# A new order for all work and loads of a state-space scan with a low-rank mixer, with 29 units of unread identity products ahead of 15 words in place of 14 ahead of 5

## The chip, the cores and the metric

One core of a Trainium2 chip runs the kernel. The engines named below are TensorE (PE, with its weight loads PEld), VectorE (DVE), ScalarE (ACT), GpSimd (POOL) and SyncE (SP), which issues all DMAs here. Each engine works off its own queue strictly in the order in which the program wrote it, and waits on semaphores for the others. The metric is the device time of one execution in microseconds; the median of several runs is given.

## The reference

Two blocks follow each other. The first is a chunked state-space scan (Mamba2 SSD) for 4 batches, 8 heads, 768 positions, head dimension 32 and state dimension 16. Its output, with the heads side by side, is the input `x` of the second, a mixer of 256 channels.

```python
# scan, per chunk of 32 positions; cum = cumsum(log a) inside the chunk
M = (Cc @ Bc.T) * exp(cum_i - cum_j) * causal
y = M @ xc + (Cc @ state) * exp(cum)
state = exp(sum(la)) * state + (Bc * decay_from_j).T @ xc
# mixer, per batch
h = x.T @ U @ V                       # rank 32, over the 768 positions
u = x + h.T
out = u + relu(u @ w_ch1) @ w_ch2     # 256 -> 1024 -> 256
```

a, B, C and x are float32. U, V and the two weights come as float64 and are turned into float32 on the chip.

## The kernel before

The scan's work is cut into twelve pairs of 128-position blocks, k = 0 to 11, three pairs to a batch. The mixer works on each batch in three blocks of 256 positions, j = 0 to 2, and takes the hidden layer in quarters, i = 0 to 3. Blocks 0 and 1 of batch 0 use plain float32 products; all others split each factor into parts near, far and both, whose products run at the faster float32r rate.

The order of everything is written out by hand in `PLANS` (lines 36 to 72). `PLANS[0]` holds the first loads. `PLANS[1]` is one list of words, and `follow` (line 1063) calls one function for each word, in order. What a word emits goes to the end of each engine's queue. So the list fixes, for every engine at once, what stands ahead of what. In words of the scan the first number is the pair minus 3 (`s-3` is pair 0, `s8` pair 11); in words of the mixer it is 1 minus the batch (`d1.0` is batch 0, block 0; `d-2.2` is batch 3, block 2).

- Loads: `B` and `X` load a pair's B with C, and its x; `L` does both for the pair of its number plus 3. `Z` loads U and V, `w0` to `w8` the words of the weights. SyncE issues them in the order of the list. The first transfer of a `B`, `X`, `L` or `w` word is also held until the last VectorE instruction written ahead of it has ended (`until`, `begin`, line 195).
- Weights: `c` (three steps for each number) turns loaded words into float32. c0 is U and V, c1 to c5 are w_ch1, c6 to c9 are w_ch2. `R` (two steps each) splits them into near, far and both.
- Scan: `A` and `K` make the decays (F, FD, kept) of all batches from the logarithms `la`. `Q` and `P` scale B and C into BC on VectorE, `E` and `D` make the decayed B (on POOL for batch 0, on VectorE after). `V` and `T` transpose BC into T and Cm; for pairs from 6 on that goes over DRAM, in two calls. `g` multiplies them, `m` and `M` mask the result on VectorE, `s` and `u` make the states. `i`, `j` and `n` add up the output, `y` copies it out, and `t` and `O` transpose it for the mixer.
- Mixer: `v` spreads U and V, `p` projects and `x` multiplies with V, `a` adds h to x (VectorE). `U` is a plain hidden quarter, `f`, `e` and `h` are the split one, `S` splits a block of u. `d` is a step of the second product; its later steps add u and store.
- `F` sets a number of identity products that the next tile in PSUM gets ahead of its own work. Nobody reads them. The tags w, x and z have 2, 3 and 3 PSUM banks.

```python
    def idle(t, n):
        while n > 0:
            m = min(n, max(t.shape[1] // P, 1), 4)
            w = min(P, t.shape[1])
            nc.tensor.matmul(out=t[:, :m * w].rearrange("p (m i) -> p m i", i=w), lhsT=ident,
                             rhs=ident[:, None, :w].to_broadcast([P, m, w]), start=True, stop=True)
            n -= m
    def bank(tag, *dims):
        t = psum.tile([P, *dims], FP32, tag=tag, name=tag, bufs=BANKS[tag])
        if fills[0]:
            idle(t if len(dims) == 1 else t.rearrange(
                {2: "p a b -> p (a b)", 3: "p a b c -> p (a b c)"}[len(dims)]), fills[0])
        fills[0] = 0
        return t
```

One unit is one product of the 128 by 128 identity with 128 columns of itself, in float32, which the profile shows as two records.

## Time and profile before

| | us |
|---|---|
| runs | 214.29, 214.87, 216.78 |
| median | 214.87 |
| profiled execution, span from first to last instruction | 212.4 |
| TensorE busy | 202.9 |
| weight loads busy | 180.9 |
| VectorE busy | 173.2 |
| ScalarE busy | 121.0 |
| POOL busy | 6.3 |

The profile is of one execution. It gives its span; the device time of that execution lies around the span, and the median of the runs is 2.5 us above it. A row of a timeline reads: start in us from the start of the span, length in us, engine, line, operation, what it writes and reads, shape, how many records were merged, and in brackets how long the engine was idle ahead of it and what it waited for. Lines of VectorE often read L170, since one helper issues them; there the tile names tell the words apart. TensorE's records overlap, so the start of the next row tells more of the time that a row takes than its own length.

### The profile page before, as it was taken

What the parts mean: (1) busy time and instruction counts of PE and PEld (TensorE: products, weight loads), DVE (VectorE), ACT (ScalarE), POOL (GpSimd) and SP (SyncE); (2) the same over time, 40 slices, a digit from 0 to 9 for tenths busy, and PEclk for the clock granted to TensorE, in tenths of its full rate; (3) what the DMA queues carried; (4) which work ended last, traced back from release to release, by engine and by line L of the source; (5) the groups of instructions that cost most, each with busy time, mean ns of one, the idle gap of its engine ahead of it and who ended that gap; (6) DMA issues with size and microseconds to landing.
All of it is one profiled execution on the core that took longest, in us unless ns stands there. A gap on an engine that the chain in (4) does not pass through costs nothing.

```text
span 212.4 us, 7511 instructions
## 1 busy us (share of the span) xinstructions
PE 202.9 (96%) x3190; PEld 180.9 (85%) x3190; DVE 173.2 (82%) x363; ACT 121.0 (57%) x279; POOL 6.3 (3%) x22
## 2 busy tenths in 40 slices
PE   7988889999999999999999999899999999999994
PEld 5765666878979997988999999589998999999993
DVE  4299979999899999999799995777986299859941
ACT  3354668489969746285588361669713565554310
POOL 4022000000000000000000000000000000000000
PEclk9999999999999999999999999999999999999999
DMA  5997799994751488356755766626510000324354
GB/s 82 138 150 160 89 246 181 190 241 121 102 71 31 79 207 130 88 83 83 108 89 94 149 143 132 112 38 122 117 52 0 0 5 0 49 32 71 49 102 99
DMA packets 120177, 21.43 MB, mean 101 GB/s; under 512 B 110096, under 2 KB 118352, under 8 KB 120144
## 3 DMA queue, kind: packets, MB, share of 16 engines
q1 hardware_dynamic: 120144, 20.95, 53.9%
q8 instruction: 25, 0.41, 0.9%
q14 instruction: 8, 0.07, 0.2%
HBM read 14.39 MB, written 6.55 MB: 99 GB/s over the span
## 4 chain that ended last, share of the span: by engine, by line
PE 75%; DVE 8%; issue 4%; DMA 4%; ACT 3%; SPq 3%; POOL 0%; POOLq 0%; DVEq 0%; ACTq 0%
PE x L846 35%; PE z L846 28%; DMA bc<-in_B_dram 4%; SPq L196 3%; DVE words L170 2%; PE x L584 2%; PE z L739 1%; PE w L803 1%; PE x L714 1%; PE x L739 1%; DVE S L170 1%; ACT yT L759 1%; PE x L815 1%; DVE o L170 1%; DVE BC L170 1%
## 5 line engine op out<-in xcount | busy, mean ns | idle before, releaser
L170 DVE SCALAR_TENSOR_TENSOR words<-words 128x512 fp32r<-128x512 f32 (+6 forms) x60 | 39.4, 669 | 2.4 <-ACT words L420 0.8
L846 PE MATMUL x<-words,w 128*128 128x256 f32 x288 | 38.1, 280 | 0.0
L846 PEld LDWEIGHTS x<-words,w 128*128 128x128 f32 x288 | 34.9, 188 | 1.6 <-issue 1.2
L846 PE MATMUL x<-u,w 128*128 128x256 f32 x240 | 34.3, 282 | 0.0
L846 PE MATMUL z<-u,w 128*128 128x256 f32 x240 | 32.7, 278 | 0.0
L851 ACT ACTIVATE x<-x 128x512 f32<-128x512 f32 (+1 forms) x27 | 15.5, 577 | 28.2 <-PE x L846 26.4
L846 PEld LDWEIGHTS x<-u,w 128*128 128x128 f32 x240 | 30.3, 188 | 0.6 <-ACT yT L759 0.2
L846 PEld LDWEIGHTS z<-u,w 128*128 128x128 f32 x240 | 29.7, 188 | 0.1
L851 ACT ACTIVATE z<-z 128x512 f32<-128x512 f32 (+1 forms) x24 | 13.7, 574 | 12.3 <-PE z L846 10.2
L846 PE MATMUL z<-words,w 128*128 128x256 f32 x144 | 19.6, 280 | 0.0
L846 PEld LDWEIGHTS z<-words,w 128*128 128x128 f32 x144 | 17.7, 188 | 0.9 <-issue 0.9
L170 DVE SCALAR_TENSOR_TENSOR words<-x,words 128x512 fp32r<-128x512 f32 x20 | 13.6, 682 | 4.5 <-ACT words L886 4.4
L170 DVE SCALAR_TENSOR_TENSOR words<-z,words 128x512 fp32r<-128x512 f32 x20 | 13.6, 682 | 2.2 <-ACT words L886 2.2
L886 ACT ACTIVATE words<-x 128x512 fp32r<-128x512 f32 x20 | 12.0, 598 | 3.3 <-PE x L846 3.2
L170 DVE TENSOR_TENSOR yT<-x,yT 128x384 f32<-128x384 f32 (+1 forms) x15 | 9.2, 613 | 5.1 <-PE x L846 2.7
L170 DVE TENSOR_TENSOR BC<-bc,F 128x512 f32<-128x512 f32 (+2 forms) x18 | 8.7, 508 | 5.4 <-DMA bc<-in_B_dram 3.0
L886 ACT ACTIVATE words<-z 128x512 fp32r<-128x512 f32 x20 | 11.8, 597 | 1.7 <-PE x L846 1.2
L170 DVE SCALAR_TENSOR_TENSOR S<-S,kept,w 128x64 f32<-128x64 f32 x40 | 11.2, 279 | 1.7
L584 PE MATMUL x<-Cm,T 32*64 32x128 f32 x192 | 11.6, 307 | 0.6 <-DVE Cm L170 0.4
L651 ACT ACTIVATE Sm<-S,slot 128x128 f32<-128x128 f32 (+1 forms) x18 | 6.0, 385 | 9.9 <-DVE S L170 9.9
L584 PE MATMUL z<-Cm,T 32*64 32x128 f32 x192 | 10.5, 307 | 0.0
L170 DVE TENSOR_TENSOR M<-x,causal 128x256 int32<-128x256 int32 x24 | 9.1, 421 | 1.6 <-PE z L584 1.6
(152 smaller groups left out, 363.5 us busy)
## 6 DMA issues: line engine op xcount, KB each, us to landing
words<-in_moe_w_ch_dram SPq DMA_DIRECT2D x7, 512.0 KB, 5.5
squares<-w1f SPq DMA_DIRECT2D x52, 64.0 KB, 1.9
x<-in_x_dram SPq DMA_DIRECT2D x24, 128.0 KB, 4.1
out_dram<-o SPq DMA_DIRECT2D x32, 64.0 KB, 2.3
bc<-in_B_dram SPq DMA_DIRECT2D x24, 64.0 KB, 3.5
bc<-in_C_dram SPq DMA_DIRECT2D x12, 128.0 KB, 3.9
T<-squares SPq DMA_DIRECT2D x6, 256.0 KB, 4.3
ytok<-squares SPq DMA_DIRECT2D x6, 256.0 KB, 3.6
```

The lines of the kernel that those rows point to most:

```text
L170: self.last = call(*args, **kwargs)
L196: op = nc.sync.dma_start(**kwargs)
L584: nc.tensor.matmul(out=g[r][cols, c], lhsT=s["T"][rows, 0, c, cols], rhs=s["Cm"][rows, :, :, ts(2 * c + p, Q)].rearrange("r v t i -> r v i ...
L651: nc.scalar.activation(s["Sm"][:, sl, v], s["S"][:, sl, ts(v, D)], AF.Copy, scale=slot[:, v, None])
L714: product = nc.tensor.matmul(out=y[r // 2][p][ts(v, H), c], lhsT=own[ts(r, Q)], rhs=s["T"][ts(r, Q), 1, :, ts(2 * c + p, Q)].rearrange("r ...
L739: product = nc.tensor.matmul(out=y[n][p][ts(v, Q), c], lhsT=x_sb[k][half, c, h], rhs=s["M"][half, h // 2, c, h % 2], start=fresh(k, n, p, ...
L759: nc.scalar.copy(out=yp[ts(1 - v, H), n, :, p], in_=y[n][p][ts(v, H)])
L803: nc.tensor.matmul(out=p[ts(n, H)], lhsT=UU[:, c].rearrange("p t r -> p (t r)"), rhs=ytok[b][:, c, ts(n, P)], start=(c == 0), stop=(c == N ...
L815: nc.tensor.matmul(out=h[q][:, :VS], lhsT=pT[rows], rhs=V4[rows], start=True, stop=True, skip_group_check=True)
L846: nc.tensor.matmul(out=t, lhsT=lhsT, rhs=rhs, start=start, stop=True, skip_group_check=True)
L851: nc.scalar.activation(t, t, AF.Copy, scale=1.0 + EPS)
L886: nc.scalar.activation(gs[j, i][0], t, AF.Relu, scale=NEAR)
```

## The change

`PLANS[1]` is replaced by another order of the same words. Every word but `F` occurs as often as before: each product, copy and transfer is still made once. The `F` words go from 5 with 14 units (5, 4, 2, 1, 2) to 15 with 29 units. Eighteen of these units stand ahead of words of batch 0 (A0, V-3.0.0, s-3, n-3, g-1, i-2, i-1, with 1, 2, 6, 1, 3, 3, 2), four ahead of g0, g1 and n2 (1, 1, 2), four ahead of x0, g3 and n5 (1, 1, 2) and three ahead of n7 and n8 (1, 2). The functions are unchanged.

```diff
--- before.py
+++ after.py
@@ -37,37 +37,36 @@
     0: (
         'B0 X0 B1 X1 B2 X2 '),
     1: (
-        'Z1 F5 A0 Q-3.0 Q-3.1 A1 Q-3.2 F4 V-3.0.0 Q-2.1 V-3.1.5 K2 D-3 g-3 Q-2.2 Q-2.0 V-2.0.2 '
-        'Z0 m-3 M-3 F2 V-2.1.2 Q-1.2 E-1.0 s-3 Q-1.0 D-2 n-3 w0 Q-1.1 V-1.0.2 u-3 F1 V-1.1.3 s-2 '
-        'w1 i-3 g-2 u-2 j-3 y-3 F2 g-1 i-2 B3 B4 B5 w2 w3 X3 w4 X4 m-2 M-2 w5 c0 c0 m-1 B6 O-3.0 '
-        'c0 M-1 w6 E-1.1 n-2 s-1 u-1 c2 v0 w7 c1 c2 j-2 i-1 y-2 j-1 n-1 c1 y-1 P0 D0 c1 T0 c2 '
-        't-2 O-1.3 P2 X5 T0 X6 w8 P1 D2 p1.0.4 p1.4.6 c3 c3 x1 a1.0 a1.1 T1 T2 T2 T1 g0 U1.0.0 '
-        'c3 c4 c4 U1.0.1 g1 m0 M0 c5 c4 m1 M1 c5 D1 s0 u0 U1.1.0 U1.1.1 U1.1.2 i0 n0 y0 c6 c6 s1 '
-        'c5 g2 c7 u1 R2 m2 c7 U1.1.3 M2 c8 c8 c7 U1.0.2 L4 U1.0.3 i1 n1 y1 c6 R1 R0 c8 R5 c9 s2 '
-        'c9 c9 n2 d1.0 L5 R6 u2 R0 d1.1 P3 S1.2 d1.0 R7 d1.0 i2 y2 R3 t1 R1 t0 R2 R5 d1.1 R4 P4 '
-        'T3 d1.0 f1.2.0 R4 T4 f1.2.2 t2 e1.2.0 f1.2.1 R6 d1.0 d1.1 D3 R3 h1.2.0 P5 d1.1 e1.2.2 '
-        'f1.2.3 e1.2.1 p0 T3 d1.2 e1.2.3 T4 T5 L6 h1.2.2 h1.2.1 R7 d1.1 x0 a0.0 a0.1 d1.2 h1.2.3 '
-        'd1.2 d1.2 d1.2 s3 g3 m3 M3 d1.2 d1.2 S0.0 d1.2 g4 m4 M4 d1.2 d1.2 d1.2 d1.2 f0.0.0 '
-        'f0.0.1 e0.0.0 T5 f0.0.2 f0.0.3 d1.2 D4 s4 e0.0.1 u3 e0.0.2 e0.0.3 L7 L8 D5 s5 h0.0.0 i3 '
-        'n3 y3 d0.0 d0.0 u4 h0.0.1 g5 h0.0.2 u5 d0.0 d0.0 d0.0 h0.0.3 d0.0 m5 M5 d0.0 P6 d0.0 T6 '
-        'n4 S0.1 i4 y4 d0.0 D6 d0.0 d0.0 d0.0 D8 f0.1.2 P7 T7 S0.2 f0.1.3 s6 n5 i5 y5 e0.1.2 '
-        'e0.1.3 f0.2.0 u6 t5 h0.1.2 f0.1.0 f0.2.1 f0.2.2 e0.2.0 f0.2.3 e0.2.1 t3 f0.1.1 e0.2.2 '
-        'e0.2.3 D7 t4 e0.1.0 h0.1.3 e0.1.1 d0.2 d0.2 d0.2 h0.2.0 h0.2.1 T6 d0.2 t3 h0.2.3 h0.1.0 '
-        'd0.1 d0.2 h0.2.2 d0.1 d0.1 d0.1 d0.2 d0.2 d0.2 h0.1.1 d0.1 t4 T7 d0.0 P8 T8 s7 u7 g6 m6 '
-        'd0.1 M6 t5 d0.1 d0.2 d0.1 d0.2 d0.2 d0.2 d0.1 d0.1 d0.1 d0.1 s8 u8 n6 i6 y6 p-1 g7 T8 '
-        'd0.2 x-1 d0.1 m7 M7 n7 a-1.0 a-1.1 S-1.0 i7 y7 g8 f-1.0.2 f-1.0.3 m8 M8 n8 i8 y8 t6 t7 '
-        'S-1.1 e-1.0.2 h-1.0.2 t6 e-1.0.3 f-1.0.0 f-1.0.1 h-1.0.3 t8 f-1.1.3 e-1.0.0 e-1.0.1 '
-        'f-1.1.0 h-1.0.0 f-1.1.1 h-1.0.1 d-1.0 S-1.2 d-1.0 f-1.1.2 d-1.0 t7 e-1.1.0 h-1.1.0 '
-        'e-1.1.1 e-1.1.2 e-1.1.3 d-1.1 d-1.0 d-1.0 h-1.1.1 d-1.0 d-1.1 d-1.0 d-1.0 h-1.1.2 d-1.1 '
-        'd-1.1 t8 d-1.1 p-2 h-1.1.3 d-1.1 x-2 a-2.0 a-2.1 d-1.1 d-1.1 S-2.0 f-1.2.0 d-1.0 d-1.0 '
-        'd-1.1 d-1.0 d-1.0 f-1.2.2 f-1.2.3 f-1.2.1 e-1.2.2 h-1.2.2 e-1.2.3 h-1.2.3 e-1.2.0 d-1.1 '
-        'f-2.0.0 h-1.2.0 d-1.1 d-1.1 f-2.0.3 e-1.2.1 h-1.2.1 S-2.1 f-2.0.2 e-2.0.0 f-2.0.1 d-1.2 '
-        'e-2.0.2 e-2.0.3 e-2.0.1 h-2.0.2 h-2.0.0 h-2.0.3 f-2.1.1 d-1.0 h-2.0.1 d-1.2 d-1.2 d-1.2 '
-        'f-2.1.0 S-2.2 d-1.2 d-1.2 d-1.2 f-2.1.2 d-1.2 f-2.1.3 e-2.1.2 d-1.2 h-2.1.2 d-1.2 d-1.2 '
-        'e-2.1.0 e-2.1.1 d-1.2 f-2.2.2 d-1.1 f-2.2.3 e-2.1.3 h-2.1.3 d-2.0 d-2.0 h-2.1.0 d-2.0 '
-        'd-2.0 d-2.0 d-2.0 d-2.0 d-2.0 d-2.2 d-1.2 e-2.2.2 h-2.2.2 e-2.2.3 h-2.2.3 f-2.2.0 d-2.0 '
-        'd-2.0 d-2.0 f-2.2.1 e-2.2.0 h-2.1.1 d-2.1 h-2.2.0 d-2.1 e-2.2.1 h-2.2.1 d-2.0 d-2.2 '
-        'd-2.1 d-2.1 d-2.1 d-2.1 d-2.1 d-2.1 d-2.2 d-2.2 d-2.0 d-2.1 d-2.1 d-2.1 d-2.1 d-2.1 '
+        'F1 A0 Q-3.0 Z1 A1 Q-3.1 Q-3.2 F2 V-3.0.0 V-3.1.5 w0 w1 Z0 K2 D-2 D-3 Q-2.1 Q-2.2 Q-2.0 g-3 '
+        'm-3 F6 s-3 u-3 V-2.0.2 V-2.1.2 B3 M-3 s-2 F1 n-3 B4 g-2 Q-1.2 w3 i-3 u-2 Q-1.0 w2 Q-1.1 B5 '
+        'j-3 w6 w4 V-1.0.2 m-2 V-1.1.3 E-1.0 X3 E-1.1 y-3 s-1 u-1 c1 F3 g-1 M-2 c0 c1 m-1 F3 i-2 M-1 '
+        'c2 n-2 c2 c0 P0 F2 i-1 X4 j-2 c0 y-2 c2 D1 c1 P1 T0 O-3.0 t-2 w5 D0 v0 j-1 n-1 p1.0.4 y-1 '
+        'O-1.3 c3 p1.4.6 c4 w7 T0 B6 x1 c4 T1 w8 c3 a1.0 a1.1 U1.0.0 F1 g0 P2 T2 T2 c3 U1.1.0 m0 M0 '
+        'T1 U1.0.1 X5 c4 c7 c5 s0 c5 F1 g1 c7 u0 m1 U1.1.1 M1 U1.1.2 i0 c5 n0 s1 y0 c6 g2 u1 U1.0.2 '
+        'c6 U1.0.3 L4 m2 R2 U1.1.3 L5 D2 t0 i1 M2 c7 c8 c6 R1 n1 D3 c8 s2 c9 d1.0 d1.1 R0 P3 F2 n2 '
+        'y1 L6 c8 c9 R3 u2 i2 R4 R6 c9 d1.1 R2 P4 S1.2 d1.0 R0 d1.1 T3 d1.0 y2 R7 R1 t2 P5 f1.2.0 R7 '
+        'T4 f1.2.2 f1.2.1 R4 e1.2.0 X6 R3 T5 d1.0 h1.2.0 R5 f1.2.3 t1 e1.2.1 e1.2.2 R6 e1.2.3 p0 '
+        'h1.2.2 R5 d1.1 T3 d1.2 d1.2 d1.2 F1 x0 h1.2.1 d1.2 h1.2.3 d1.2 d1.2 T5 d1.2 a0.0 a0.1 d1.2 '
+        's3 F1 g3 D5 m3 d1.2 d1.2 S0.0 T4 d1.2 d1.2 f0.0.0 f0.0.1 M3 g4 u3 e0.0.0 m4 d1.0 M4 f0.0.2 '
+        'e0.0.1 L7 f0.0.3 D4 d1.1 e0.0.2 e0.0.3 d1.2 h0.0.0 i3 s4 n3 L8 h0.0.1 h0.0.2 h0.0.3 y3 S0.1 '
+        'd0.0 u4 d0.0 g5 d0.0 d0.0 d0.0 d0.0 m5 f0.1.3 M5 P6 d0.0 S0.2 d0.0 s5 n4 i4 y4 d0.0 d0.0 u5 '
+        'T6 d0.0 d0.0 f0.2.2 P7 T7 F2 n5 D6 i5 s6 P8 y5 f0.1.2 e0.2.2 D7 f0.2.0 f0.2.3 e0.2.0 e0.1.2 '
+        'f0.2.1 e0.2.3 f0.1.0 e0.2.1 u6 e0.1.3 t5 t3 h0.2.2 t4 f0.1.1 h0.2.0 h0.2.3 e0.1.0 d0.2 d0.2 '
+        'e0.1.1 T6 h0.2.1 d0.2 d0.2 h0.1.2 d0.2 h0.1.0 d0.1 t5 D8 T7 d0.1 T8 d0.2 d0.1 d0.1 d0.2 '
+        'h0.1.3 h0.1.1 t4 d0.0 s7 g6 d0.1 d0.1 d0.2 m6 d0.1 M6 d0.1 d0.2 d0.2 s8 u7 T8 n6 d0.2 t3 '
+        'd0.1 u8 d0.2 d0.2 d0.1 d0.1 d0.1 d0.1 i6 y6 p-1 g7 x-1 m7 M7 F1 n7 i7 a-1.0 a-1.1 S-1.0 y7 '
+        't6 g8 f-1.0.2 m8 f-1.0.1 M8 F2 n8 t7 i8 S-1.1 t6 y8 e-1.0.2 f-1.1.0 f-1.0.0 f-1.0.3 t8 '
+        'h-1.0.2 e-1.0.0 e-1.0.1 f-1.1.1 f-1.1.2 t8 t7 h-1.0.0 h-1.0.1 d-1.0 e-1.0.3 e-1.1.0 e-1.1.1 '
+        'h-1.0.3 f-1.1.3 d-1.0 h-1.1.1 d-1.0 e-1.1.2 d-1.1 h-1.1.2 d-1.0 e-1.1.3 h-1.1.3 d-1.0 d-1.0 '
+        'p-2 d-1.1 x-2 h-1.1.0 d-1.1 d-1.1 a-2.0 d-1.0 S-1.2 f-1.2.0 d-1.0 a-2.1 f-1.2.1 d-1.0 d-1.0 '
+        'd-1.0 d-1.0 e-1.2.0 S-2.0 e-1.2.1 d-1.1 h-1.2.1 d-1.1 f-1.2.3 h-1.2.0 f-1.2.2 f-2.0.0 d-1.1 '
+        'e-1.2.2 e-1.2.3 d-1.0 f-2.0.2 d-1.1 h-1.2.2 e-2.0.0 d-1.2 d-1.2 d-1.2 d-1.2 S-2.1 d-1.2 '
+        'd-1.1 e-2.0.2 h-1.2.3 f-2.0.1 d-1.1 h-2.0.2 h-2.0.0 d-1.1 f-2.0.3 S-2.2 f-2.1.0 e-2.0.1 '
+        'h-2.0.1 e-2.0.3 d-1.2 d-1.2 f-2.1.2 d-1.2 e-2.1.0 f-2.1.1 d-2.2 h-2.0.3 d-1.2 d-1.1 d-1.2 '
+        'd-1.2 e-2.1.1 d-1.2 e-2.1.2 f-2.2.3 f-2.1.3 d-2.0 d-2.0 h-2.1.0 d-2.0 f-2.2.2 e-2.1.3 d-2.1 '
+        'd-2.0 d-2.1 d-2.0 h-2.1.1 h-2.1.2 d-2.1 d-2.1 d-1.1 h-2.1.3 d-2.0 f-2.2.1 f-2.2.0 e-2.2.2 '
+        'd-1.2 d-2.0 d-2.0 e-2.2.0 e-2.2.1 h-2.2.0 e-2.2.3 d-2.0 d-2.1 d-2.0 d-2.0 d-2.1 d-2.1 '
+        'h-2.2.1 h-2.2.3 d-2.1 d-2.2 d-2.2 d-2.0 d-2.1 d-2.1 d-2.1 d-2.0 h-2.2.2 d-2.1 d-2.1 d-2.2 '
         'd-2.2 d-2.2 d-2.2 d-2.2 d-2.2 d-2.2 d-2.2 d-2.2 d-2.2 d-2.2 '),
 }
```

## The prediction

> **What bounds the kernel now.** I read the page first, then busy time by stage, then the queues of single engines around each wait.
>
> ```profile
> PE 202.9 (96%) x3190; PEld 180.9 (85%) x3190; DVE 173.2 (82%) x363; ACT 121.0 (57%) x279; POOL 6.3 (3%) x22
> ...
> PE 75%; DVE 8%; issue 4%; DMA 4%; ACT 3%; SPq 3%; POOL 0%; POOLq 0%; DVEq 0%; ACTq 0%
> ```
>
> TensorE (PE) is busy for 96% of the span and holds 75% of the chain that ended last. The order of its queue therefore decides most of the time. But 25% of that chain lies elsewhere, and the stages tell where.
>
> ```profile
> core 0 of [0], span 212.4 us
> core 0: us, PE busy (x) PEld busy (x) DVE busy (x) ACT busy (x) POOL busy (x), PEclk, DMA share, GB/s
> 0.00:34.40 34.40, 29.62 (x629) 21.98 (x630) 25.32 (x79) 18.57 (x49) 6.27 (x22) 1.00 0.86 147
> 34.40:60.90 26.50, 25.87 (x489) 21.07 (x488) 24.82 (x58) 19.38 (x45) 0.00 (x0) 1.00 0.72 151
> 60.90:104.00 43.10, 42.88 (x678) 38.13 (x677) 41.20 (x79) 28.63 (x68) 0.00 (x0) 1.00 0.60 101
> 104.00:131.00 27.00, 27.00 (x476) 26.12 (x477) 23.52 (x49) 15.02 (x35) 0.00 (x0) 1.00 0.63 117
> 131.00:145.00 14.00, 13.29 (x378) 10.59 (x360) 9.81 (x25) 9.02 (x28) 0.00 (x0) 1.00 0.49 94
> 145.00:212.40 67.40, 64.24 (x572) 62.97 (x570) 48.51 (x78) 30.41 (x58) 0.00 (x0) 1.00 0.27 52
> ```
>
> TensorE idles 34.40 - 29.62 = 4.8 us before the mixer's first plain products (U1.0.0), 0.63 us up to 60.9, 0.22 us up to 104, nothing up to 131, 0.71 us around the turn to the last batch, and 3.2 us in the rest. In the second stage VectorE (DVE) is nearly as full, 24.82 of 26.50 us. A new order of the same work can win in the first stage, a little in the second, and around 131 to 145. Elsewhere it can only add. The 3.2 us of the rest are mostly the store behind the last product, which both orders have; both also end on ten d-2.2. The profiled span is 212.4 us and the median of the runs 214.87, so I put 2.5 us around the span and carry differences.
>
> **The opening.** F5 stands ahead of A0 now, F1 after.
>
> ```profile
> 4.09 0.36 ACT L335 ACTIVATE la<-la 128x192 f32<-128x192 f32 x1 [2.01 <-DVE la L170]
> ```
>
> ```profile
> 3.79 2.34 PE L140 MATMUL w<-ident 128*128 128x128 f32 x10
> 5.93 0.85 PE L365 MATMUL w<-la,ref 128*128 128x192 f32 x2
> ```
>
> The ten identity products are F5: two records a unit, (5.93 - 3.79) / 5 = 0.43 us a unit. The logarithms that A0 multiplies are ready at 4.09 + 0.36 = 4.45, yet A0 starts at 5.93. With one unit (3.79 + 0.43 = 4.22) it starts at 4.45, so A0, the first decays F and the first scaled BC come 1.48 us sooner.
>
> ```profile
> 9.95 0.29 DVE L170 TENSOR_TENSOR BC<-bc,F 128x128 f32<-128x128 f32 x1 [1.59 <-DMA bc<-in_B_dram]
> 10.16 0.60 DVE L170 TENSOR_SCALAR Cm<-w,slot 128x128 f32<-128x128 f32 x2
> ```
>
> Next in line is a blocked queue. Q-2.1 waited 1.59 us for pair 1's B, and the Cm of V-3.1.5, which was ready to run, stood behind it on VectorE; g-3 stood behind that Cm on TensorE. After, V-3.1.5 and K2 come ahead of Q-2.1, so that wait holds nothing that g-3 needs. On POOL it is the other way: D-2, which needs the same B, now stands ahead of D-3, so s-3 cannot run before some 11 us. F6 stands in that gap and costs nothing there.
>
> ```profile
> 14.92 0.39 PE L140 MATMUL x<-ident 128*128 128x128 f32 x2
> 15.15 0.38 PE L498 MATMUL x<-ident,BC 128*128 128x128 f32 x2
> ```
>
> From here a unit takes 15.15 - 14.92 = 0.23 us, half of what it took at 3.79. I price all later units by this row. The 15 extra units are 3.5 us of TensorE in all.
>
> **To the first plain products.**
>
> ```profile
> 29.84 1.29 DVE L170 TENSOR_TENSOR BC<-bc,F 128x512 f32<-128x512 f32 x2 [1.36 <-DMA bc<-in_B_dram]
> 31.05 0.42 DVE L170 TENSOR_TENSOR bd<-bc,FD 128x256 f32<-128x256 f32 x1
> 31.39 0.76 DVE L170 TENSOR_SCALAR words<-words 128x512 int32<-128x512 int32 x2
> 32.06 0.55 DVE L170 TENSOR_TENSOR yT<-x,yT 128x384 f32<-128x384 f32 x1
> ```
>
> ```profile
> 22.45 0.58 PE L1012 MATMUL x<-UV,ident 128*32 128x192 f32 x8
> ```
>
> ```profile
> 30.04 0.59 PE L815 MATMUL x<-V,pT 32*128 32x384 f32 x2 [0.37 <-ACT pT L808]
> ```
>
> a1 (the adds from 32.06) had x1's products by about 31 (30.04, and three more rows like it), but VectorE was behind: P2 had waited 1.36 us for B5, and P1, D2 and c3 followed. After, P2 stands behind a1, and that wait goes. What is late next is x1 itself. c0's last step, which makes U and V, now follows u-1, c1's, c2's first steps and P0, some 2.5 us of VectorE work by the rows of these forms. So v0 (22.45) comes 1 to 3 us later even after the better opening, and p1 and x1 behind it stay near 30.4 (estimate: n-1 and y-1, which p1 also needs, come some 0.5 us late). a1 then starts at about 31.2, against 32.06, and one x1 word later U1.0.0 follows without g0 ahead of it. VectorE has the same work done at that point (P2 short, c4's first step ahead), so both engines are about 0.85 us ahead; F1 and g0 cost TensorE 0.2 us of it. I take **-0.7 us**, between 0 (x1 fully as late as v0) and -2.8 us (1.48 + 1.36, all carried).
>
> The loads move past each other on SP's queue: w6 and w4 now go ahead of X3, and X4, w5, w7, w8 each wait for the last VectorE instruction written ahead of them (P0, P1, c4), with all later loads behind.
>
> ```profile
> 27.28 2.22 SPq L196 DMA_DIRECT2D x<-in_x_dram  x2
> ```
>
> ```profile
> 38.81 0.43 PE w L619 x31
> ```
>
> X3 was issued by 29.5 and its first user, s0, ran at 38.8, so it has 9.3 us in hand. Two words of 512 KB at the stage's 151 GB/s are 6.9 us. It fits by 2.4 us less the flight; I take 0, and up to +2 for the range.
>
> **To 60.9.**
>
> ```profile
> 57.42 1.30 DVE L170 SCALAR_TENSOR_TENSOR words<-words 128x512 f32<-128x512 f32 x2 [0.80 <-ACT words L420]
> 58.76 0.69 DVE L170 SCALAR_TENSOR_TENSOR o<-words 128x512 f32<-128x512 f32 x1
> 59.37 0.91 DVE L170 SCALAR_TENSOR_TENSOR S<-S,kept,w 128x64 f32<-128x64 f32 x3
> ...
> 61.52 0.69 DVE L170 TENSOR_TENSOR BC<-bc,F 128x512 f32<-128x512 f32 x1
> ```
>
> ```profile
> 59.51 1.78 PE L846 MATMUL x<-words,o 128*128 128x256 f32 x7 [0.16 <-DVE o L170]
> ```
>
> The second halves of d1.0 and d1.1 wait for c9's last step (58.76 + 0.69 = 59.45), and TensorE starts on it at 59.51 with 0.16 us idle. After, D3 (0.42), P3 (0.69) and u2 (0.91) stand ahead of that step: 2.0 us. The start gains 0.85 and the 0.80 us wait on ScalarE can close, so c9 ends near 59.8. TensorE gets there no sooner: it has t0 and i2 (some 1.1 us, work that came after before) and three units (g1, n2: 0.7 us) on the way. Net of the moved work: -0.7 + 0.7 - 0.16 = **-0.2 us** at this point.
>
> **From 60.9 to 131.** R, S, f, e and h keep the distance from what they read, as far as sums of their rows tell. Units ahead of x0, g3 and n5 are four, 0.9 us, and TensorE has 0.22 us of idle time for them: **+0.7 us**, between 0 and +0.9.
>
> **131 to 145.**
>
> ```profile
> 131.86 0.64 ACT L651 ACTIVATE Sm<-S,slot 128x96 f32<-128x96 f32 x2 [4.21 <-DVE S L170]
> 133.13 0.27 ACT L761 COPY yT<-x 128x128 f32<-128x128 f32 x1 [0.63 <-DVE o L170]
> ...
> 134.68 0.27 ACT L808 COPY pT<-w 128x128 f32<-128x128 f32 x1
> ```
>
> ```profile
> 135.00 0.59 PE L815 MATMUL x<-V,pT 32*128 32x384 f32 x2 [0.61 <-ACT pT L808]
> ```
>
> u8 waited on VectorE, y6's copies came behind it on ScalarE, then pT, and TensorE idled 0.61 us for pT. After, some eight d words lie between u8 and y6, so ScalarE is free for y6 when i6 ends: **-0.6 us**. The three units ahead of n7 and n8 (0.7 us) go into what is left of the 0.71 us of idle time and the gaps at n7 and g8: 0, at most +0.7. The rest of the order is products without gaps on both sides: 0, or up to +1 where h-2.2.2, now ahead of d-2.1's end, makes the last rows wait.
>
> **Sum:** -0.2 + 0.7 - 0.6 = -0.1 us, so 214.87 - 0.1 = **214.8 us**. What the opening wins, the units in the full stages give back.
>
> A rule against this change: the Trainium skill, "TensorE: Matmul & The Clock Gate" (HAM oscillation), has the array fall to half rate only after idle gaps of about 3.4 us. TensorE's idle time here is 0.71 us at most in any whole stage from 34.4 to 145. By that rule units past the opening buy no clock, and only their cost stands; the sum has it so already.
>
> **Rivals.**
> *The waits go and nothing comes back (faster).* The opening's 1.48 and P2's 1.36 us are carried whole, pT's 0.61 goes, and all units fall into idle time: 214.87 - 3.45 = 211.4 us. For it: VectorE sets the pace up to 60 (24.82 of 26.50 busy), and weight loads leave TensorE slack there (21.07 of 26.50). Against it: c0 comes later, and stages with PE at 27.00 of 27.00 have no room.
> *The units are paid (slower).* The 11 units from g0 on all stand in front of products that could have run: 11 x 0.23 = 2.5 us, and the opening's gain is lost at v0, so 214.87 + 2.5 = 217.4 us. For it: idle time from 34.4 to 145 is 1.56 us in all, less than their sum. Against it: they are written ahead of words that wait for VectorE or ScalarE. It decides from 34.4 on, where TensorE is the last to be ready.
> *The clock comes late.* The unit's 0.43 us at 3.79 and 0.23 us at 14.92 show products at half rate in the opening, while the page's clock column says 1.00. With four units fewer there, TensorE could stay at that rate until about 10 us. A0 is such work (its two records end 0.85 us after they start), and A1, V-3 and K2 ahead of g-3 are about four times as much; half of that, 1.7 us (estimate), comes on top and the gain of 1.48 is gone. That gives 214.87 - 0.1 + 0.7 = 215.5, up to 216 us. Against it: A0, A1 and F2 move up into the room that F5 leaves. The same page (What's actually happening) gives one busy window of about 3.4 us as what releases the clock; by that rule it hangs on whether 1.4 to 6.9 us stays full, and the trace of before agrees, with products from 1.4 us on, 0.43 us a unit at 3.79 and 0.23 at 14.92.
>
> **Chances.** Forecast 0.45, the faster rival 0.26, the slower 0.23, the late clock 0.06. The forecast's own range is 213 to 216.8, from the ends of its terms. The eight-in-ten range reaches to both rivals, 211.0 to 218.2 us; the top takes in a late X3 or tail on the slower rival. About 1% (2.1 us) is what a measurement of this kernel tells from no change; the three runs lie 1.2% apart. Faster by over 1%: the first rival and 0.03 of the forecast's lower end, 0.29. Slower: the second and 0.05 of its upper end, 0.28. Within: 0.43.
>
> **What would show it.** Right: A0's matmul at about 4.5 us and units at 0.23 us from 7 or 8 us on; a1's first add at 31 to 31.5; c9's last step near 59.8; no idle time for pT near 135. Wrong: units of 0.43 us still at 9 us (late clock); a1 below 30 (faster rival) or v0 after 26 with a1 no sooner than now (slower); idle time on TensorE for a DMA of x near s0; new idle time on TensorE past 145, where there is none now, which no term of mine pays for.

## The result, and the profile after

The changed kernel takes 222.88 us (median of 4 runs, 221.61 to 225.09), the kernel before in the same runs 215.81 us (214.29 to 216.78). The ratio is 1.031, 95% interval 1.024 to 1.039: slower. (Ratios, here and below, leave out the slow runs, those over 1.5% above the fastest of their kernel.) The forecast was 214.8 us, no change, with a range from 211.0 to 218.2. The measured time lies above that range.

The page of the changed kernel, on an execution of 223.57 us (line numbers are one lower than before, so L845 is the mixer's products and L139 the identity units):

```profile
span 221.9 us, 7581 instructions
...
PE 212.2 (96%) x3220; PEld 189.6 (85%) x3220; DVE 174.3 (79%) x363; ACT 122.5 (55%) x279; POOL 6.2 (3%) x22
...
PEclk9999999999999999999999998899999999999999
...
PE 91%; DVE 3%; DMA 3%; issue 1%; ACT 0%; POOL 0%; DVEq 0%; POOLq 0%; SPq 0%
```

TensorE's share is 96% as before, but of a longer span. Its busy time grew by 212.2 - 202.9 = 9.3 us, and that is nearly the whole difference of the spans (221.9 - 212.4 = 9.5 us). In sum TensorE waits as long as before, though not at the same places. The question is why the same products, with 15 more units, keep it busy 9.3 us longer. A new sight is the dip in PEclk two thirds along.

To see where the time goes when the order differs, I put both traces on one scale: each word of the list (F left out) is worth the least time that it took on TensorE in any profile of this study, and the lag is how much later a kernel reaches the same amount of work done. This is worked out from TensorE's rows, not a view of the profile. It is good to a few tenths, but only to about 1 us at 20 and 54 us, where a wait falls inside a word. In us, at the times of the kernel before:

```
                             20    32    54    90   128   134   144   180   end   span
changed kernel              3.0   3.2   2.1   2.9   2.9   6.3   7.3   8.3   9.4  221.9
changed kernel once more    2.9   3.0   1.9   2.7   3.2   4.0   4.8   5.9   6.7  219.4
```

There are three places: 2 to 3 us by the first plain products, 1.6 to 4.4 us at the turn to the last batch (128 to 144), and 2 us spread evenly over the last 65 us. From 54 to 128 us little is lost.

**The opening.** TensorE's rows of the changed kernel at the decays, and then those of the kernel before:

```profile
4.47 1.00 PE L364 MATMUL w<-la,ref 128*128 128x192 f32 x2
...
8.12 0.85 PE L379 MATMUL z<-la,after 128*128 128x192 f32 x2
8.76 0.74 PE L381 MATMUL z<-la,onward 128*128 128x160 f32 x2
...
11.69 1.60 PE L139 MATMUL w<-ident 128*128 128x128 f32 x12
```

```profile
8.83 0.49 PE L380 MATMUL z<-la,after 128*128 128x192 f32 x2
9.16 0.43 PE L382 MATMUL z<-la,onward 128*128 128x160 f32 x2
```

A0 starts at 4.47, as forecast. But K2's first product takes 8.76 - 8.12 = 0.64 us to the next, against 0.33 before: half rate, still at 8 to 10 us, while the clock column of that stretch reads 1.00. That column can't tell here: the trace's record of the clock begins at 7.2 us in the kernel before and at 10.7 us in this execution, and ahead of its record the column reads 1.00. VectorE gets K2's result no sooner:

```profile
11.07 0.53 DVE L169 TENSOR_TENSOR own<-z,mine 128x352 f32<-128x352 f32 x1 [1.32 <-PE z L389]
```

Before, that step began at 10.68. The 1.48 us are gone again by K2, and then F6 stands at 11.69 for 1.53 us (s-3 follows at 13.22). The gap ahead of s-3 in which F6 was to cost nothing is not there: g-3, late with the clock, ends at 11.76.

**The turn.** SyncE's queue, then TensorE, then ScalarE of the changed kernel:

```profile
127.28 2.84 SPq L966 DMA_DIRECT2D out_dram<-o  x4
130.29 0.50 SPq L531 DMA_DIRECT2D T<-squares  x1
130.83 0.53 SPq L531 DMA_DIRECT2D ytok<-squares  x1
```

```profile
137.14 2.83 PE L802 MATMUL w<-ytok,UU 128*64 128x128 f32 x24 [2.38 <-DMA ytok<-squares]
```

```profile
140.00 0.27 ACT L807 COPY pT<-w 128x128 f32<-128x128 f32 x1 [2.42 <-PE w L802]
```

The fetch of pair 6's transposed output, the second t3, is issued at 130.83. In the kernel before it is the first of the three fetches t3, t4, t5, at 118.85:

```profile
118.85 1.13 SPq L532 DMA_DIRECT2D ytok<-squares  x2
```

Now it is the last, behind d0.0's stores and T8's fetch. TensorE idles 2.38 us for it, and p-1 then takes 2.83 us for its 24 products, where such a group took 1.53 us at 76.65 before. The stretches show why (times, PE busy, and after the counts the granted clock):

```profile
134.00:136.00 2.00, 0.76 (x27) 0.47 (x26) 1.84 (x3) 1.27 (x4) 0.00 (x0) 1.00 0.15 29
136.00:138.00 2.00, 0.86 (x8) 0.89 (x10) 0.00 (x0) 1.52 (x7) 0.00 (x0) 0.75 0.65 102
138.00:140.00 2.00, 2.00 (x28) 1.67 (x31) 0.00 (x0) 0.00 (x0) 0.00 (x0) 0.50 0.63 96
140.00:142.00 2.00, 2.00 (x38) 1.16 (x38) 1.06 (x4) 0.27 (x1) 0.00 (x0) 0.89 0.41 65
```

After the idle time the granted clock falls to 0.50, so in this execution the fetch costs twice. The half clock is not what makes the kernel slow, though: two of the four runs show a granted clock of 0.998 and 1.00 over the whole span and still take 221.61 and 222.18 us.

**The last 65 us.** The same 16 products of 256 columns near the end, in the kernel before and in the changed one (the next row's start shows how long they really take):

```profile
205.45 1.98 PE L846 MATMUL z<-w,words 128*128 128x256 f32 x16
207.26 1.07 PE L846 MATMUL x<-w,words 128*128 128x256 f32 x8
```

```profile
214.74 2.05 PE L845 MATMUL z<-w,words 128*128 128x256 f32 x16
216.62 1.10 PE L845 MATMUL x<-w,words 128*128 128x256 f32 x8
```

That is 1.81 us against 1.88 us, 113 against 117.5 ns a product, at a granted clock of 1.00 in both. From 144 us to the end, where such products fill TensorE, the lag grows by 9.4 - 7.3 = 2.1 us.

### The profile page after: what moved, and what is told of

It is laid out like the page before. It is cut to its first block, busy times and chain, and to the rows that moved or that the text cites. A ratio compares the mean times of both kernels' runs of the same rounds, so it can differ in the third digit from the quotient of the medians.

```text
span 221.9 us, 7581 instructions
## 1 busy us (share of the span) xinstructions
PE 212.2 (96%) x3220; PEld 189.6 (85%) x3220; DVE 174.3 (79%) x363; ACT 122.5 (55%) x279; POOL 6.2 (3%) x22
## 4 chain that ended last, share of the span: by engine, by line
PE 91%; DVE 3%; DMA 3%; issue 1%; ACT 0%; POOL 0%; DVEq 0%; POOLq 0%; SPq 0%
PE x L845 36%; PE z L845 28%; PE x L583 3%; DMA ytok<-squares 3%; PE x L139 3%; PE w L802 3%; PE w L618 2%; PE x L713 2%; PE x L814 2%; PE x L738 2%; PE z L738 2%; PE w L139 1%; DVE S L169 1%; PE w L497 1%; PE z L713 1%; PE z L583 1%
## 5 line engine op out<-in xcount | busy, mean ns | idle before, releaser
L845 PE MATMUL x<-words,w 128*128 128x256 f32 x288 | 40.4, 283 | 0.0
L845 PEld LDWEIGHTS x<-words,w 128*128 128x128 f32 x288 | 36.3, 189 | 1.3 <-issue 1.0
L845 PE MATMUL x<-u,w 128*128 128x256 f32 x240 | 34.3, 284 | 0.0
L845 PE MATMUL z<-u,w 128*128 128x256 f32 x240 | 33.5, 282 | 0.0
L845 PEld LDWEIGHTS x<-u,w 128*128 128x128 f32 x240 | 30.4, 189 | 0.7 <-ACT yT L758 0.2
L845 PEld LDWEIGHTS z<-u,w 128*128 128x128 f32 x240 | 30.4, 189 | 0.1
L845 PE MATMUL z<-words,w 128*128 128x256 f32 x144 | 20.6, 282 | 0.0
L845 PEld LDWEIGHTS z<-words,w 128*128 128x128 f32 x144 | 18.3, 189 | 0.9 <-issue 0.9
L169 DVE SCALAR_TENSOR_TENSOR S<-S,kept,w 128x64 f32<-128x64 f32 x40 | 11.2, 279 | 3.2 <-PE w L618 1.6
L139 PE MATMUL x<-ident 128*128 128x128 f32 (+2 forms) x38 | 9.4, 353 | 1.7 <-POOL ident masks.py:199 1.4
L583 PE MATMUL x<-Cm,T 32*64 32x128 f32 x192 | 10.6, 312 | 0.1
L583 PE MATMUL z<-Cm,T 32*64 32x128 f32 x192 | 10.2, 312 | 0.4 <-DVE M L169 0.4
L169 DVE TENSOR_TENSOR u<-yT,u 128x512 fp32r<-128x512 f32 x10 | 6.9, 688 | 4.4 <-ACT u L839 4.4
```

The costliest lines, as they stand in the source:

```text
L169: self.last = call(*args, **kwargs)
L583: nc.tensor.matmul(out=g[r][cols, c], lhsT=s["T"][rows, 0, c, cols], rhs=s["Cm"][rows, :, :, ts(2 * c + p, Q)].rearrange("r v t i -> r v i ...
L845: nc.tensor.matmul(out=t, lhsT=lhsT, rhs=rhs, start=start, stop=True, skip_group_check=True)
```

## The experiments

Each kernel was timed beside the kernel before. Words of the lists are quoted; "..." leaves words out.

### The fetch, the first 60 us, and the units

```diff
- ... h0.1.2 d0.2 h0.1.0 d0.1 t5 D8 ... s8 u7 T8 n6 d0.2 t3 d0.1 u8 ...
+ ... h0.1.2 d0.2 h0.1.0 d0.1 t3 t5 D8 ... s8 u7 T8 n6 d0.2 d0.1 u8 ...
```

> The changed kernel with one word moved: the second t3, which fetches pair 6's transposed output and stood last of the three fetches, now stands ahead of the second t5. Theory F (the fetch sets the turn to the last batch): in the changed kernel SyncE reached that fetch at 130.83 us, behind d0.0's stores and T8's fetch, TensorE idled 2.38 us for it and then ran p-1 at a lower granted clock (slices of .50 and .89). With the fetch issued some 10 us sooner p-1's products should follow without that wait: 2.4 us less for sure, up to 4.5 with the clock kept, so 218.4 to 220.5 us against 222.9. Rival U (what is late there is ScalarE and the units, not the fetch): TensorE waits about as long for pT and the copies of y6, and the time stays within 1 us of 222.9.

222.78 us (219.0 to 225.4; before 217.02). The times settle little: the one run with a clock of 0.998 takes 219.0 us, the other three, with 0.95 to 0.98, 222.5 us and more. The fetch is issued at 123.5 us, and p-1 has no wait in front of it:

```profile
136.24 1.56 PE L802 MATMUL w<-ytok,UU 128*64 128x128 f32 x24
```

Theory F holds for the wait, and p-1 takes 1.56 us again, though the clock granted in this execution is 0.95 from 10 us to the end. Rival U is not empty: right behind p-1 TensorE waits 0.7 us for y6's copies and 0.6 us for pT. Between 128 and 134 us the lag grows by 0.5 us here against 3.4. Over all profiles it grows by 0.8 to 3.4 us there (mean 1.9 of six) with the late fetch and by 0 to 0.7 (ten) with the early one. This run's time does not show the saving; the runs without the units from g0 on, below, show it better.

The second run has the words up to c9's last step in the order and with the units of the kernel before, the rest as changed.

> All words that the changed order has up to c9's last step, but in the order and with the units of the kernel before; everything after that as in the changed order. Theory O (the opening costs about what it shows at c9's last step): that step starts at 57.42 us before and at 60.46 in the changed kernel, so about 3 us less, 219 to 221 us. Rival: half of that is made up by 90 us anyway (f0.0.0 is only 1.3 us late in the changed kernel), and the gain at the end is 1.3 us or less, 221.5 to 222.5. The fetch of pair 6 near 131 to 137 us keeps its wait in both.

223.29 us, ratio 1.029 (1.024 to 1.034). Its lag is 0.8 us at 44 us, where the changed kernel has 2.5, so the old opening is better by 1.7 us; but 4.1 us at 60. It lost them at g2, where TensorE stood still for 1.27 us, and at the seam, where i2 waited 1.77 us for ScalarE. The run leaves the question open.

```diff
- 'm-3 F6 s-3 ... s-2 F1 n-3 ... c1 F3 g-1 M-2 c0 c1 m-1 F3 i-2 ... P0 F2 i-1 ...'
+ 'm-3 s-3 ... s-2 n-3 ... c1 g-1 M-2 c0 c1 m-1 i-2 ... P0 i-1 ...'
```

> The changed kernel without the 15 units ahead of s-3, n-3, g-1, i-2 and i-1; F1 and F2 at the start and the 11 units from g0 on stay. Theory P (these units stand in front of work that could run): F6 held s-3 back to 13.29 us, the two F3 took 0.92 us each; c0's last step comes 2 to 3.5 us sooner than 26.01, v0 sooner than 28.58, and the end 1.5 to 3 us sooner, 220 to 221.4. Rival I (they stand in idle time, and keep the clock up): c0 and v0 stay within 0.5 us, or the granted clock in the first 30 us is lower and products take longer, and the time is 222.9 or above.

224.27 us, ratio 1.036 (1.029 to 1.044). Rival I is right, and strongly. The lag is 7.1 us at 32 us, and the clock shows it (stretches of this run):

```profile
10.00:13.00 3.00, 1.41 (x36) 0.96 (x36) 2.81 (x9) 0.58 (x3) 1.42 (x2) 0.85 1.36 122
13.00:16.00 3.00, 2.71 (x120) 2.28 (x119) 2.79 (x11) 1.35 (x6) 0.78 (x2) 0.50 1.18 186
16.00:20.00 4.00, 1.42 (x28) 0.95 (x21) 0.63 (x2) 0.00 (x0) 1.22 (x3) 0.50 0.77 173
20.00:24.00 4.00, 3.61 (x46) 2.48 (x46) 2.70 (x10) 2.24 (x8) 0.39 (x1) 0.50 0.71 89
```

Without the units the clock is at half from 13 to 30 us. They are no waste in this order. The fall comes after g-3, where TensorE idles 1.62 us for s-3, the place that F6 fills in the changed kernel.

The fourth run takes out the other 11 units, from g0 on.

> The changed kernel without the 11 units ahead of g0, g1, n2, x0, g3, n5, n7 and n8. The prediction priced four of them at 0.7 us and the others at next to nothing, its slower rival all 11 at 0.23 us, 2.5 us. First reading (next to nothing: the last batch starts late because of a fetch, not because of units): 222 to 223 us, p-1 still waits for the fetch. Second reading (all are paid): 220.4 us, with every word from c9 on 0.5 us and more sooner and y5 2 us sooner than 110.50.

219.0 us, ratio 1.013 (1.008 to 1.018), 3.9 us less than the first measurement of the changed kernel and 1.5 less than its second (below). At 128 us its lag is 2.2 us where the changed kernel's is 2.9 and 3.2. So the units ahead of g0 to n5 cost 0.7 to 1 us by the profiles. In the profiled run p-1 waits 1.84 us for the fetch, and half clock follows for 10 us; eight of the ten runs show a granted clock of 0.997 or more and so no such fall.

### Units and order apart

The first two runs have the changed order with the units of before (F5 A0, F4 V-3.0.0, F2 V-2.1.2, F1 V-1.1.3, F2 g-1), the second of them with the fetch early. The third has the old order with the change's 29 units. The fourth is the changed kernel with the fetch early and without the 11 units from g0 on.

> The changed order of words, but the identity units of the kernel before: F5 ahead of A0, F4 ahead of V-3.0.0, F2 ahead of V-2.1.2, F1 ahead of V-1.1.3, F2 ahead of g-1, and no others. Theory U (units and one fetch make up the loss): no units from g0 on saves 2.4 us as in the run without them, up to 3.5 by the time the units take on TensorE (0.31 to 0.54 us a place); the opening gets its clock as early as in the kernel before, so the lag of 2 us at 20 to 60 us shrinks to 1 or less; the wait of 2.4 us for pair 6's fetch stays, with or without 1.6 us at half clock after it. That is 2.5 to 5 us above the kernel before of the same runs. Rival W (the order itself is worse in the opening, since c0 and v0 come late): v0 is still near 28 us, the lag at 60 us stays above 2, and the time is 5 to 7 us above the kernel before.

> As the run before it, and the second t3 ahead of the second t5. Theory U: TensorE does not wait for the fetch near 134 to 137 us, the clock stays up there, 2.4 to 4 us less than with the units of before alone: within 1.5 us of the kernel before. Rival W: 2 us and more above the kernel before, the lag standing from the opening on.

> The order of the kernel before, with the change's 29 units ahead of the same 15 words. It tells the price of the units without the new order. Theory U: units from g0 on 2.4 to 3.5 us, the opening about as late as in the changed kernel at 20 us (F6 and the clock, 1 to 2 us), no wait for the fetch: 3.5 to 5.5 us above the kernel before. Rival W (the order is at fault, units lie beside waits): 0 to 1.5 us above the kernel before. Rival H (the 18 units of the opening only suit the changed order): the clock falls to half somewhere in the first 30 us, 6 us and more above.

> The changed kernel with the second t3 moved as above and without the 11 units from g0 on; the opening with its 18 units stays. Both gains should add, since they lie in different places: 2.4 (units) + 2.4 (fetch) + up to 1.6 (clock kept at 137 to 141 us) = 4.8 to 6.4 us less than the changed kernel, 216.5 to 218 us where that one takes 222.9; what is left above the kernel before, 1 to 2.5 us, is the opening. Rival: n7 and n8's units covered a wait for the copies of y6 and y7, which then shows up on TensorE near 140 us, and less than 4 us are gained.

224.91 us (ratio 1.038, 1.027 to 1.048), 223.21 (1.025, 1.012 to 1.038), 218.64 (1.012, 1.001 to 1.022) and 218.33 (1.006, 1.000 to 1.011), before 216.41. Theory U fails for the first two and so does W in its mechanism: v0 is late, but the loss is clock. In the first, TensorE stands still at g-2 for nothing that the profile shows, and the clock column follows:

```profile
PE x L583 <- issue: 4.1, 1, 4.1
```

```profile
PEclk9995559999999999999999999999999999999998
```

Fourteen units that keep the clock in the old order do not in the new one. The fourth run goes about as expected: without a wait for the fetch and at full clock it is 2.5 us behind at 144 us, some 2 us of it from before 90 us. Against the run with the units alone taken out (ratio 1.013, ten runs each) the earlier fetch gives 1.006, some 1.5 us. TensorE still waits for pT here, as in the kernel before (its waits from 128 to 152 us):

```profile
PE x L814 <- ACT pT L807: 0.6, 1, 0.6
```

```
                             20    32    54    90   128   134   144   180   end   span
new order, old units        6.9   9.0   7.5   7.6   8.2   9.5   9.5  10.3  11.1  223.9
 and fetch early            1.2   4.9   5.3   5.6   5.9   6.4   9.3   9.7   9.7  222.4
old order, 29 units         1.8   0.7   1.4   1.9   2.4   2.4   3.5   3.5   3.5  215.9
new order, 18, fetch early  3.2   3.4   1.6   1.9   2.4   2.4   2.5   2.9   2.9  215.6
old order, 18 units         2.4   1.2   0.8   0.7   0.2   0.2   0.4   1.3   2.4  214.8
old order, 24 units         2.4   1.3   0.7   1.7   1.0   1.2   1.2   1.2   1.2  213.6
```

The last two lines belong to the next group: the old order with the opening's units alone, with F1 and F2 or with F5 and F4 at the start.

> The order of the kernel before with the change's 18 units of the opening in place of its own 14, and none from g0 on. With all 29 units that order took 218.64 us at a granted clock of 1.00 in each run, and its profile was 0.7 us behind the kernel before at 30 us and 3.5 us behind at the end. Theory C (units in the opening keep the clock, units later only cost): the later 2.8 us go, the opening's 0.7 us stay, the clock stays up where runs of the kernel before show 0.99: a span near 213 us, 214.5 to 215.7 us, 0.5% below the kernel before of the same runs. Rival T (what kept the clock were the units ahead of n7 and n8, at the turn to the last batch): most runs show 0.99 again and take 216 to 217.5 us.

> As the run before it, with F5 ahead of A0 and F4 ahead of V-3.0.0 as in the kernel before, so 24 units in the opening. The profiles so far put the late clock (F1) and the early A0 at the same point by K2: 10.67 us with 1 and 2 units against 10.68 with 5 and 4. Theory C: the time is within 0.5 us of the run with 18 units. Rival E (the early clock is worth more than the units take): 1 us less. Rival X (seven more units are paid): 0.7 us more and above.

> The changed order with the second t3 moved up, and of the units only F1 ahead of A0, F2 ahead of V-3.0.0 and F6 ahead of s-3. It asks which of the opening's units the clock hangs on. Theory S (F6 alone closes the gap in which the clock would fall): full clock in the opening, the 9 units left out take 2.7 us of TensorE less, v0 1 to 2 us sooner than 28.8, the time 1 to 2 us below the 218.3 us of the run with all 18. Rival R (TensorE must be kept busy all along 15 to 30 us): the granted clock falls to half somewhere between 13 and 30 us as it did without any of them, 221 to 224 us.

> The changed kernel once more, word for word, for a second profile beside the others of these runs. The wait of 2.4 us for pair 6's fetch and half clock after it should be there again. From y8's copy to the end the first profile took 72.2 us, its 256-column products 117.8 ns apart, where the kernel before took 69.95 at 113.4 ns. If the spacing belongs to the order of the words, it is 117.8 again; if it falls differently from one execution to the next, 113.4 is as likely, and the span is 2 us shorter. The time: 221.5 to 223.5 us, 2.5 to 3.5% above the kernel before.

The old order with 18 units takes 215.53 us against 216.44, ratio 0.998 (0.993 to 1.002): as fast as the kernel before, not shown faster. With 24 units it is 217.66, 1.007 (1.003 to 1.011); its lag equals that of 18 up to 54 us, and then TensorE stood still 1.5 us at a d1.0. In these two, K2's step on VectorE begins at 11.26 and 10.68. At 20 us both lag 2.4: what F1 wins at A0, the clock takes.

The 18 units of the opening, in place of 14, cost 0.7 us at 54 us in the old order. The changed order with the same 18 units is at 1.6 there and at 1.9 at 90. So some 0.7 us are units and 0.9 to 1.2 the order. The times agree that the order costs: with the same 18 units and no late fetch the new order has the ratio 1.006 and the old one 0.998.

F6 alone gave 223.44 us, 1.022 (1.012 to 1.033): theory S falls. Its clock held until 26 us and was 0.59 and 0.56 from 26 to 30 us, after TensorE had idled 2.2 us at j-2.

The changed kernel once more took 220.47 us (219.38 to 225.27; before 216.44), 1.016 (1.006 to 1.027), less than at first, and its trace shows where it differs. p-1 waits 1.18 us and not 2.38, the clock stays at 1.00 at the turn, and near the end the rows below appear. (The view puts the 1.18 us down to VectorE's `o`, whose step ends at 136.11. But in the run of 218.33 us p-1 starts 1.2 us before that same step ends, so it does not need it; the fetch, issued at 131.41, is the likelier cause.)

```profile
206.60 1.58 PE L845 MATMUL z<-words,w 128*128 128x256 f32 x12
208.01 0.63 PE L845 MATMUL x<-w,words 128*128 128x256 f32 x4
...
212.14 1.98 PE L845 MATMUL z<-w,words 128*128 128x256 f32 x16
213.95 1.07 PE L845 MATMUL x<-w,words 128*128 128x256 f32 x8
```

Twelve products in 1.41 us, 117.5 ns each; 5.5 us later sixteen in 1.81, 113 ns each. The spacing does not belong to the order of the words.

### What the opening hangs on

```diff
- ... u-1 c1 F3 g-1 M-2 c0 c1 m-1 F3 i-2 M-1 c2 n-2 c2 c0 P0 F2 i-1 X4 j-2 c0 y-2 ... D0 v0 j-1 ...
+ ... u-1 c0 c0 c0 c1 F3 g-1 M-2 c1 m-1 F3 i-2 M-1 c2 n-2 v0 c2 P0 F2 i-1 X4 j-2 y-2 ... D0 j-1 ...
```

```diff
- ... g-3 m-3 F6 s-3 u-3 V-2.0.2 V-2.1.2 B3 M-3 ...
+ ... g-3 V-2.0.2 m-3 M-3 V-2.1.2 F6 s-3 u-3 B3 ...
```

Both edits start from the run of 218.33 us; the third run has both.

> The run with the fetch moved up and no units from g0 on (218.3 us, 2.0 us behind the kernel before at 54 us of its profile), with the three c0 ahead of the first c1 and v0 behind n-2, about where the kernel before has them. It asks whether v0, 28.8 us there against 22.04 before, is what holds the first plain products back. Theory V: v0 comes 4 us sooner, p1, x1 and U1.0.0 1 us sooner and all after it, 217 to 217.5 us. Rival Q (something else is late with it: VectorE does the same work in another order, and the chain from V-2 over g-1 to y-1 sets x1): v0 moves, U1.0.0 stays within 0.3 us of 36.9, the time within 0.5 us of 218.3.

> The same run with V-2.0.2, M-3 and V-2.1.2 ahead of F6 and s-3, the order of the kernel before there. In the changed order V-2's transposes stand behind F6 and s-3 (T copied at 14.08 to 14.31 us against 12.81) and all of pairs 1 and 2 after them (V-1.0.2 at 19.1 against 15.12). Theory Q: V-2 is 1.3 us sooner, U1.0.0 and the words after it 0.7 to 1.3 us sooner, 217 to 217.6 us. Rival V: pair 1 is sooner but U1.0.0 stays within 0.3 us of 36.9, since v0 is as late. Rival R: with V-2 gone from behind F6 the gap that F6 filled opens elsewhere and the granted clock falls to half.

> Both moves together. If they are two parts of the same lag, 1.3 us is gained in all: U1.0.0 near 36.2 us or before, 216.5 to 217.2 us, level with the kernel before within 0.3%. If the order's loss lies in neither, 218 us or above.

224.94 us (1.039, 1.029 to 1.049), 222.84 (1.029, 1.018 to 1.040) and 224.64 (1.041, 1.033 to 1.049). None of the theories holds. In the first, the clock came early: K2's first two products stand 0.32 us apart and VectorE has its step at 8.85 us, 2.4 us sooner than in the run it starts from, with the same words up to there. Then TensorE stands still at g-2 and the clock goes (stretches, then the wait):

```profile
13.00:16.00 3.00, 2.38 (x107) 1.68 (x107) 2.75 (x11) 1.24 (x5) 0.70 (x2) 1.00 1.14 195
16.00:20.00 4.00, 1.39 (x39) 1.20 (x39) 0.93 (x4) 0.00 (x0) 1.29 (x3) 0.84 0.71 168
20.00:24.00 4.00, 4.00 (x47) 2.92 (x50) 2.71 (x9) 2.47 (x8) 0.55 (x1) 0.50 0.77 98
```

```profile
PE x L583 <- issue: 2.5, 1, 2.5
```

Moving V-2 made TensorE wait 1.18 us for Q-2.0's result before the transposes, and F6 then cost its 1.5 us where it had covered that wait before. So F6 did stand in a gap, if only in part, and not in the one that the prediction had, ahead of s-3.

These standstills come at fixed places of TensorE's stream: at g-2 after 221 of its matmul records each time (no opening units; c0 early; old units), though these kernels have different units ahead of g-2, and at g2 after 856, 855 and 855 (old opening; old units with early fetch; F6 alone). That points to instructions that come late, and the profile's instruction queue fits that. In these six standstills, and in three shorter ones at 220, 855 and 1111 records, TensorE starts again 1.3 to 1.6 us after the end of a 16 KB transfer on that queue: at 18.80 after 17.25 without the opening's units, at 19.96 after 18.35 with the old units. The next three runs move the loads Z0, w0 and w1 behind n-3 and g-2, to clear the DMA queues at 14 to 17 us: from old units with early fetch, from c0 early, and from the run of 218.33 us.

```diff
- ... V-3.1.5 w0 w1 Z0 K2 ... F1 n-3 B4 g-2 Q-1.2 w3 ...
+ ... V-3.1.5 K2 ... F1 n-3 Z0 B4 w0 g-2 Q-1.2 w1 w3 ...
```

> The changed order with the units of before and the fetch of pair 6 moved up (223.2 us), and the loads Z0, w0 and w1, which the change put ahead of K2, moved behind n-3 and g-2. In the profiles in which the clock fell to half in the opening, TensorE first stood still for 1.1 to 4.1 us with nothing to wait for that the profile shows, five times out of eight inside g-2 or s-2 at 15 to 20 us, at the same places of its instruction stream, and the profile's instruction queue brought its first 16 KB at 13 to 18 us, when w0, w1 and Z0 fill the DMA queues. Theory I (TensorE runs out of instructions there, since their transfer shares the queues with the loads): no such gap of over 0.5 us at g-2 and s-2, the clock at 1.00 up to 24 us. Whether the later gap at j-2 (24.5 us) goes too is open; if it does, 217 to 219 us. Rival K (the clock falls by itself where TensorE has little to do): the clock falls to half between 12 and 30 us as before, 222 us and above.

> The run with the three c0 and v0 early (224.9 us; TensorE stood still for 2.5 us at g-2, clock at half from 17 to 30 us), with the same three loads moved behind n-3 and g-2. Theory I: no stand of over 0.5 us at g-2, the clock stays up, and v0 is near 24 us: 216.5 to 218.5 us, level with or below the 218.3 us of the run without the early c0. Rival K: the clock falls again, 222 us and above. Rival L (c0 needs Z0, w0's words come later and hold c1): VectorE waits for the loads instead, and v0 and U1.0.0 stay where they are with c0 late.

> The run with the fetch moved up and no units from g0 on (218.3 us), with Z0, w0 and w1 moved behind n-3 and g-2 and nothing else. Its profile had no stand at g-2 and full clock, but 7 of its 10 runs only did. Theory I: the clock now is 1.00 in each run, U1.0.0 within 0.5 us of 36.9, 217 to 218 us. Rival L: c1 waits for w0, U1.0.0 is 0.5 us later or more, 218.5 us and above.

225.55 us (1.044, 1.036 to 1.052), 226.08 (1.042, 1.033 to 1.052) and 224.87 (1.041, 1.033 to 1.048). No run stood still at g-2 or s-2 for more than 0.8 us, but Rival L came true and hides the rest. The last run, its waits and its stretches:

```profile
PE z L583 <- DVE M L169: 5.1, 1, 5.1
DVE words L169 <- DMA words<-in_moe_w_ch_dram: 4.9, 1, 4.9
```

```profile
20.00:25.00 5.00, 0.77 (x8) 0.37 (x6) 0.10 (x2) 0.29 (x2) 0.51 (x1) 0.78 0.86 155
25.00:30.00 5.00, 4.17 (x110) 3.32 (x110) 4.06 (x13) 2.68 (x6) 0.00 (x0) 0.54 0.94 259
```

c1 waits 4.9 us for w0, the mask for g-1 stands behind it on VectorE, TensorE waits 5.1 us for that mask, and half clock follows. The early place of w0 in the changed order is needed by its early c1. What makes the instructions late stays open: the standstills went with the loads, but the run that the last kernel starts from had none either.

## Why the prediction was wrong, step by step

- **A0 1.48 us sooner:** right at A0 (4.47), void at K2. The late clock, the rival at 0.06, is what happened in this stage. With F5 ahead of A0 the trace's record of the clock begins by 7.3 us in all five profiles that have one; with F1 it begins at 9.1 to 11.2 us in ten of fourteen. In the old order 18 and 24 units, with F1 or F5 ahead of A0, lag alike from 20 to 54 us, so this part is worth nothing, not 1.48.
- **Unit price 0.23 us:** too low for small groups. From the first unit to the next word's start it is 0.31 to 0.42 us for F1, 0.54 to 0.63 for F2, 0.85 for F3. All F words take 9.5 us of TensorE after and 4.5 before, so the added ones 5.0 us and not 3.5. F6, priced at nothing, held s-3 back: it starts at 13.22 behind F6 and at 11.59 without the opening's units.
- **-0.7 us at the first plain products:** failed. U1.0.0's activation starts at 36.67 against 35.93, a1 at 33.99 against 32.06, with v0 5.5 us late on TensorE (27.99 against 22.45) where I had 1 to 3. Of the lag of about 2 us some 0.7 are units and 0.9 to 1.2 the order. Which words make that was not found: moving c0 or V-2 cost the clock.
- **-0.2 us at 60.9:** failed with it; c9's last step ends at 61.78 + 0.69 = 62.47 and not near 59.8:

```profile
61.78 0.69 DVE L169 SCALAR_TENSOR_TENSOR o<-words 128x512 f32<-128x512 f32 x1
```

- **+0.7 us from 60.9 to 131:** right within its bounds. The lag grows by 0.2 to 0.6 us from 60 to 128.
- **-0.6 us from 131 to 145:** the step that failed worst in the profile, and by omission. I followed u8, y6 and pT and never costed the second t3, a DMA that the order moved behind two others and the stores on SyncE's queue. It cost a wait of 2.38 us and then half clock, +3.4 us by 134 and 0.4 more by 139; in the second profile of the same kernel 1.18 us and no half clock, +0.8. The -0.6 us itself would not have come either: with the fetch early, TensorE waits 0.6 us for pT, as before.
- **Units ahead of n7 and n8 for nothing:** wrong by about 0.5 us. The lag grows by 0.5 to 0.6 us from 139 to 144 with them (changed kernel, both profiles, and the old order with 29 units) against 0.1 to 0.2 without (fetch early with 18 units, old order with 18).
- **Tail 0 to +1:** no word of the order shows a cost there. The 2.1 us of the profile go with the spacing of 117.5 ns, which a second profile of the same kernel left before its end and the old order with 18 units shows too.

The slower rival, 217.4 us, had the sign, and its price for the units from g0 on, 2.5 us, was nearer than my 1.4 (0.7 for g0, g1 and n2, 0.7 for x0, g3 and n5, nothing for the rest). By the profiles they cost 1 to 1.5 us in the new order and 3.1 in the old one (3.5 less 0.4 us of lag at 144); by the times they are worth 1.5 to 3.9 us in the new order and 3.1 in the old one. Its second half, the opening's gain lost at v0, is what the profile shows, with part of it lost to the late clock before that. Step by step, the ratios go from 1.031 and 1.016 (two measurements of the change) to 1.013 without the units from g0 on, 1.006 with the fetch early as well, and 0.998 with the old order back and the same 18 units of the opening. So units, fetch and order each have a part, of 1 to 4 us for the first, some 1.6 us for the second and 1.8 for the third, each good to about 1 us; how much of the rest is the spacing and the clock of single executions stays open.

The prediction cited the Trainium skill, "TensorE: Matmul & The Clock Gate" (HAM oscillation), for idle gaps of about 3.4 us as what costs the clock, and concluded that units buy nothing past the opening. This case disagrees: 0.50 came after gaps of 2.38 and 1.84 us, while 1.18, 1.5 and 1.7 us left the clock at 1.00. The measurement decides; the last section shows what it goes by here. Even inside the opening the rule was used too narrowly: the 15 units ahead of s-3 to i-1, whose worth for the clock I left out, kept 13 to 30 us at full rate, as the run without them shows.

## What to carry to other kernels

When a list is reordered, follow every DMA word to its place on the issuing queue and compare issue and need, even where the engines' own chain looks shorter. Price idle time on TensorE twice where it may be 2 us long: once as the wait, once as the half clock that some executions show after it. Filler products are judged with the order around them: take them out of that order before calling them cost or gain.
